# A transformer-style block on one core: the second matrix product runs three half steps behind the first, its passes in a new order, and the splitting of operands moves from GpSimd to ScalarE and VectorE

## The chip, the cores and the metric

The kernel runs on one core of a Trainium2 chip. The time is what one execution takes on the device, in microseconds (us). The engines of a core run side by side, each with its own queue of instructions in a fixed order, and wait for each other by semaphores: TensorE (PE, matrix products into PSUM), VectorE (DVE), ScalarE (ACT), GpSimd (POOL) and SyncE (SP, which only issues DMAs here). In a profile PEld stands for the loading of weights into TensorE.

## The reference

Two blocks follow each other. The first is an attention with a polynomial sketch: for 4 batches and 4 heads of 1088 tokens with 32 features, queries and keys are projected with S1 and S2 (8 x 32), the two projections multiplied pairwise to 64 features, and

```python
kv = np.einsum('bhsf,bhsd->bhfd', k_p, v)
z = np.sum(k_p, axis=2)
num = np.einsum('bhsf,bhfd->bhsd', q_p, kv)
den = np.einsum('bhsf,bhf->bhs', q_p, z)[..., None] + 1e-06
return (num / den)
```

Its result, as 4352 tokens of 128 features, is the input x of the second block, a mixture of E = 4 experts with F = 1024 hidden features, all in float32:

```python
p = domain_probs / (domain_probs.sum(-1, keepdims=True) + 1e-09)
for e in range(E):
    h = np.maximum(x @ w1[e], 0.0)
    out += p[:, e:e + 1] * (h @ w2[e])
```

## The kernel before, in words

The 4352 tokens are cut into 11 chunks (`CHUNKS`, line 71): 128, 448, 512 six times, 320, 256 and 128. A chunk takes 16 steps; a step `i` is a chunk `m` and a number `kq` that stands for an expert `e` and a pair `f` of blocks of 128 hidden features. So an expert takes four steps, and a step has two half steps, `j` = 0 and 1, each with one block of hidden features. The main loop (line 1084) goes through the steps and writes the order of all engines' instructions by hand; nothing reorders it later. Chunk 0 and the last are "plain" (whole fp32 products, tokens on the other side of the array). Chunk 1 is "whole": plain fp32 products for all four experts.

From chunk 2 on an fp32 product is put together from faster passes. Tokens and weights are split into rounded parts a and b and a correction d, held in the type fp32r. The first product of a half step, in `first`, has three passes: xa with wa (line 911), xb with wb (912), and, after ScalarE has scaled the sum in PSUM by 1 + 2^-12 (913), xd with wd (931). The third pass stands in `third`, one half step later, behind the first two passes of the next half step, so that ScalarE's scaling lies beside other passes. In what follows these three passes, two of a half step and the third of the one before, are called a trio. `third` also makes the hidden values. Of the even blocks (`in_three`) it makes three parts: ha by ScalarE (935), hb and hd by VectorE (936 and 937; the code calls the last one hc). Of the odd blocks it makes a single fp32 tile hid by ScalarE (943).

The second product, in `second`, multiplies the hidden values of an even block in three passes, ha and hb into one PSUM bank (o0, lines 994 and 995) and hd into another (o1, 1001), and of an odd block in one fp32 product into o1 (1001 too). That fp32 product counts as two instructions in the profile and takes as long as about four passes. `second` runs two steps behind `first` (`LA`), that is four half steps: `between` puts it after the trios. In the last step of an expert (`closing`) both halves are put after the first trio, so that the expert's end, `close`, comes early, and nothing stands after the second trio.

`close` calls `gather` (1022): ScalarE copies o0 out of PSUM with a scale (1030), VectorE adds o1 (1031), GpSimd multiplies by the gates of the tokens and adds to the chunk's total (1035 to 1038). o0 and o1 have one buffer each, so the next expert's first pass into a bank waits for that copy. ev, ob and total have one buffer each too.

The splits of weights (`weight_parts`, `second_weight_parts`) are spread over steps 16 to 39 by `to_part`, those of the tokens of a chunk (`token_parts`) are made in step 12 of the chunk before. ScalarE makes rounded copies (706, 717, 734, 758) and GpSimd subtracts (710).

The attention of the later batches runs beside all this in small pieces (`front`), most of them on VectorE. `work` hands them out evenly after each half step's first product, by what the next chunks need; at step 12 of a chunk what is still missing for the next one is made at once.

Of the kernel before, what the change touches and what calls it, by code (L numbers as in the profile page):

```python
# [8 lines left out]
F32 = mybir.dt.float32  # L9
# [15 lines left out]
def kernel(  # L25
# [673 lines left out]
    wb = cpool.tile([P, E, F], F32R, name="wb")  # L699
    wd = cpool.tile([P, E, F], F32R, name="wd")  # L700

    def scaled(tag, w, scale, dtype=F32):

        t = mpool.tile([P, CW], F32, tag=tag, bufs=1, name="tw")[:, :]
        t = t[:, 0 : w.shape[-1]]
        nc.scalar.activation(t.bitcast(dtype), w, ACTF.Copy, scale=scale)
        return t

    def minus(out, in0, in1):
        nc.gpsimd.tensor_tensor(out=out, in0=in0, in1=in1, op=ALU.subtract)  # L710

    def weight_parts(e):

        HF = F // 2
        for c in (slice(0, HF), slice(HF, F)):
            w, a, b, d = (x[:, c] for x in (w1_of[e], wa[:, e], wb[:, e], wd[:, e]))
            nc.scalar.activation(a, w, ACTF.Copy, scale=4096.0 * NEAR)
            minus(b, scaled("ob", w, 4096.0), a.bitcast(F32))
            yield
            minus(d, b.bitcast(F32), scaled("ev", w, NEAR, F32R))  # L720
            yield


# [3 lines left out]
    def second_weight_parts(e):  # L727

        w = w2_of[e, 0]
        vab = cpool.tile([P, 2, KS * NK * DM], F32R, tag=f"w1_{e}", name="vab")  # L730
        a, b = vab[:, 0], vab[:, 1]
        minus(b, scaled("ob", w, 4096.0), scaled("ev", w, 4096.0 * NEAR, F32R))
        yield
        nc.scalar.activation(a, w, ACTF.Copy, scale=NEAR)
        d = cpool.tile([P, KS * NK * DM], F32R, tag=f"w2_{e}0", name="vd")[:, :]
        minus(d, b.bitcast(F32), a.bitcast(F32))
        w2_parts[e] = a, b, d
        yield

# [13 lines left out]
    def token_parts(m):  # L753

        n = CHUNKS[m]
        xa, xb, xd_ = (mpool.tile([P, CW], F32R, tag=f"x{i}", name=f"x{i}") for i in "abd")
        ((x, _, _),) = placed(START[m], n)
        nc.scalar.activation(xa[:, 0:n], x, ACTF.Copy, scale=R12 * NEAR)
        minus(xb[:, 0:n], x, scaled("ew", x, NEAR, F32R))
        minus(xd_[:, 0:n], xa[:, 0:n].bitcast(F32), xb[:, 0:n].bitcast(F32))  # L760
        xparts[m] = xa, xb, xd_

    def start():

# [76 lines left out]
    def plain(m):  # L841
        return m in (0, NC - 1)

    def whole(m):
        return m == 1

    begun_hp, made_hp = {}, {}

# [12 lines left out]
    def first(i, work, between=None):  # L861
# [29 lines left out]
            work()  # L891
            return
        hid[i] = []
        if whole(m):
            ((x, _, _),) = placed(START[m], n)
            for j in range(2):
                hp = psum(ps_h, "h")[:, 0:n]
                nc.tensor.matmul(hp, w1_of[e][:, P * (2 * f + j) : P * (2 * f + j + 1)], x, start=True, stop=True)
                u = hidden()[:, 0:n]
                nc.scalar.activation(u, hp, ACTF.Relu)  # L900
                hid[i].append(u)
                work()
                if between and j == 0:
                    between(0)
            return
# [39 lines left out]
    def second(i, j=None):  # L945
# [4 lines left out]
        if plain(m):  # L950
# [27 lines left out]
        if whole(m):  # L978
# [7 lines left out]
        if f == 0 and j in (0, None):  # L986
            acc[m, e] = psum(ps_o, "o0"), psum(ps_o, "o1")
        o0, o1 = (o[:, 0:n] for o in acc[m, e])
        for j in range(2) if j is None else (j,):
            k = 2 * f + j  # L990
            if in_three(k):
                w = slice(DM * split_at(k), DM * (split_at(k) + 1))
                (va, vb, vd), (ha, hb, hc) = w2_parts[e], hd[j]
                nc.tensor.matmul(o0, va[:, w], ha, start=(k == 0), stop=False)  # L994
                nc.tensor.matmul(o0, vb[:, w], hb, start=False, stop=(k == FB - SK + KS - 1))  # L995
                o1_next.append((vd[:, w], hc))
            else:
                o1_next.append((second_weight(e, k), hd[j]))
            if k:
                for x, (w, h) in enumerate(o1_next):  # L1000
                    nc.tensor.matmul(o1, w, h, start=(k == 1 and x == 0), stop=(k == FB - 1 and x == len(o1_next) - 1))  # L1001
                o1_next.clear()

    o1_next = []

    def turn_back(m, src):

# [14 lines left out]
    def gather(m, e):  # L1022

        n = CHUNKS[m]
        ev = mpool.tile([P, CW], F32, tag="ev", bufs=1, name="ev")
        o0, o1 = acc.pop((m, e))
        if o0 is None:
            nc.scalar.copy(ev[:, 0:n], o1[:, 0:n])
        else:
            nc.scalar.activation(ev[:, 0:n], o0[:, 0:n], ACTF.Copy, scale=1.0 + R12)  # L1030
# [37 lines left out]
        begun_hp[i] = psum(ps_h, "h")  # L1068
        half_columns(i, begun_hp[i], 0)
    to_part = {}  # L1070
    for e in range(E):
        for at, parts_of in ((NQ + 4 * e, weight_parts(e)), (NQ + 8 + 4 * e, second_weight_parts(e))):
            for x in range(4):
                to_part.setdefault(at + x, []).append(parts_of)
    ending = iter(())

    def close(i):

        nonlocal ending
        ended = gather(steps[i][0], steps[i][1] // NP)  # L1080
        next(ended)
        ending = chain(ending, ended)

    for i in range(len(steps) + LA):
        if i < len(steps):
# [15 lines left out]
                    credit[0] -= 1  # L1101
                    piece()

            parted = i >= LA and not plain(steps[i - LA][0]) and not plain(m)
            closing = parted and steps[i - LA][1] % NP == NP - 1

            def between(j):

                if closing:
                    second(i - LA)  # L1110
                    close(i - LA)
                else:
                    second(i - LA, j)

            first(i, work, between if parted else None)
            for parts_of in to_part.get(i, ()):
                next(parts_of, None)
            if kq == NQ - 4 and 0 < m < NC - 2:
                while have[0] < START[m + 1] + CHUNKS[m + 1]:
                    piece()  # L1120
                token_parts(m + 1)
            if i == 2:
                gate_quotients()
            elif i == 5:
# [12 lines left out]
        if i >= LA:  # L1137
            parted = i < len(steps) and parted
            mm, kk = steps[i - LA]
            if parted and closing:  # L1140
                continue
            second(i - LA, 1 if parted else None)
            if kk % NP == NP - 1 and not plain(mm):
                close(i - LA)
            else:
                next(ending, None)

# [1 line left out]
_INS = ["q", "k", "v", "S1", "S2", "moe_domain_probs", "moe_w1", "moe_w2"]  # L1149
# [26 lines left out]
```

## Time and profile before

| what | us |
|---|---|
| time, median of 3 runs | 485.01 (484.96 to 485.11) |
| the profiled execution's own time | 485.2 |
| its span, first to last instruction | 483.4 |
| PE busy | 471.4 (98%) |
| VectorE busy | 327.2 (68%) |
| ScalarE busy | 331.2 (69%) |
| GpSimd busy | 141.9 (29%) |
| chunk 1, by the first products' starts | 29.4 to 81.0 |
| chunk 2 | 81.0 to 138.5 |
| chunks 3 to 7 | 138.5 to 404.6 |
| chunks 8 and 9 | 404.6 to 464 |

A row of the timeline has the start and the length in us, the engine, the line of the code, the instruction, what it writes and reads, and in brackets how long the engine stood idle before it and which instruction ended that. The ends of matmuls are modelled and overlap; their starts show the pace. The granted TensorE clock was full throughout.

### The profile page before, as it was taken

The numbers are of one execution on the slowest core, as the hardware profiler recorded it, in microseconds if no ns is written. First come the engines' busy times: TensorE is split into PE (matmuls) and PEld (weight loads), VectorE is DVE, ScalarE is ACT, GpSimd is POOL, SyncE is SP. The second block draws the span as 40 slices with busy tenths as digits, with TensorE's granted clock in tenths as the row PEclk, the third lists the DMA queues.
The fourth block names the chain that finished last, engine by engine and source line by source line (L and its number), as shares of the span: only waits on it lengthen the run. The fifth ranks groups of instructions, "written<-read, shape, count | busy, mean of one in ns | idle before, by whom it ended". The sixth has DMA issues, their size and how long they took to land.

```text
span 483.4 us, 8071 instructions
## 1 busy us (share of the span) xinstructions
PE 471.4 (98%) x2845; PEld 330.8 (68%) x2845; DVE 327.2 (68%) x615; ACT 331.2 (69%) x696; POOL 141.9 (29%) x149
## 2 busy tenths in 40 slices
PE   8999999989999999999999999999999999999997
PEld 5965555656666676666666676667666666888987
DVE  6833250696877769687887669597877686765652
ACT  4366676876857777676857777676877686888841
POOL 5134478432222124211322124212331032232120
PEclk9999999999999999999999999999999999999999
DMA  7827204411101212411103210013102100120710
GB/s 225 273 69 159 66 22 87 97 42 23 44 23 49 45 44 65 118 24 41 41 23 65 45 33 24 22 17 45 38 24 58 29 14 15 34 57 22 244 34 18
DMA packets 45472, 29.19 MB, mean 60 GB/s; under 512 B 26264, under 2 KB 40952, under 8 KB 45432
## 3 DMA queue, kind: packets, MB, share of 16 engines
q1 hardware_dynamic: 45416, 28.68, 23.6%
q8 instruction: 22, 0.36, 0.3%
q14 instruction: 18, 0.15, 0.1%
q10 hardware_dynamic: 16, 0.00, 0.0%
HBM read 24.42 MB, written 4.24 MB: 59 GB/s over the span
## 4 chain that ended last, share of the span: by engine, by line
PE 66%; DVE 6%; ACT 5%; issue 2%; ACTq 0%; DVEq 0%
PE o L1001 23%; PE h L931 10%; PE h L912 8%; PE h L911 8%; PE o L994 5%; PE o L995 5%; ACT h L913 3%; PE n L226 2%; PE h L226 2%; PE o L226 1%; DVE qp L535 1%; DVE hd L937 1%; DVE kp L425 1%; PE f L666 1%; DVE hb L936 1%
## 5 line engine op out<-in xcount | busy, mean ns | idle before, releaser
L913 ACT ACTIVATE h<-h 128x512 f32<-128x512 f32 (+2 forms) x256 | 138.0, 539 | 100.6 <-PE h L912 91.6
L936 DVE SCALAR_TENSOR_TENSOR hb<-h,ha 128x512 fp32r<-128x512 f32 (+2 forms) x128 | 80.8, 631 | 92.3 <-ACT ha L935 91.8
L911 PE MATMUL h<-xa,wa 128*128 128x512 f32 (+2 forms) x256 | 140.5, 549 | 0.0
L1001 PE MATMUL o<-hid,w_sb 128*128 128x512 f32 (+2 forms) x256 | 119.2, 547 | 0.0
L937 DVE SCALAR_TENSOR_TENSOR hd<-ha,hb 128x512 fp32r<-128x512 f32 (+2 forms) x128 | 98.8, 772 | 8.4
L931 PE MATMUL h<-xd,wd 128*128 128x512 f32 (+2 forms) x256 | 98.3, 384 | 3.2 <-ACT h L913 1.5
L912 PE MATMUL h<-xb,wb 128*128 128x512 f32 (+2 forms) x256 | 94.2, 368 | 0.0
L1037 POOL TENSOR_TENSOR ev<-ev,gate 128x512 f32<-128x512 f32 (+3 forms) x27 | 31.3, 1159 | 153.8 <-DVE ev L1031 153.1
L943 ACT ACTIVATE hid<-h 128x512 f32<-128x512 f32 (+2 forms) x128 | 70.2, 548 | 0.2 <-PE h L931 0.2
L935 ACT ACTIVATE ha<-h 128x512 fp32r<-128x512 f32 (+2 forms) x128 | 69.9, 546 | 0.0
L911 PEld LDWEIGHTS h<-xa,wa 128*128 128x128 f32 x256 | 48.2, 188 | 30.1 <-issue 18.6
L912 PEld LDWEIGHTS h<-xb,wb 128*128 128x128 f32 x256 | 48.3, 189 | 29.3 <-issue 23.6
L931 PEld LDWEIGHTS h<-xd,wd 128*128 128x128 f32 x256 | 48.0, 188 | 23.7 <-ACT h L913 16.0
L1001 PEld LDWEIGHTS o<-hid,w_sb 128*128 128x128 f32 x256 | 45.9, 188 | 8.1
L1001 PE MATMUL o<-hd,vd 128*128 128x512 f32 (+2 forms) x128 | 48.3, 378 | 2.7 <-DVE ev L1031 2.7
L994 PE MATMUL o<-ha,vab 128*128 128x512 f32 (+2 forms) x128 | 50.6, 395 | 0.0
L995 PE MATMUL o<-hb,vab 128*128 128x512 f32 (+2 forms) x128 | 47.4, 370 | 0.0
L1038 POOL TENSOR_TENSOR total<-total,ev 128x512 f32<-128x512 f32 (+3 forms) x27 | 35.4, 1313 | 2.1
L535 DVE TENSOR_TENSOR qp<-qa,qb 64x512 f32<-64x512 f32 (+5 forms) x44 | 33.1, 753 | 1.0
L1035 POOL TENSOR_TENSOR total<-ev,gate 128x512 f32<-128x512 f32 (+3 forms) x9 | 10.5, 1163 | 70.3 <-issue 34.0
L1001 PEld LDWEIGHTS o<-hd,vd 128*128 128x128 f32 x128 | 24.0, 187 | 9.3 <-DVE ev L1031 4.5
L984 PE MATMUL o<-hid,w_sb 128*128 128x448 f32 x64 | 28.9, 544 | 0.0
(150 smaller groups left out, 545.4 us busy)
## 6 DMA issues: line engine op xcount, KB each, us to landing
gate<-gates SPq DMA_DIRECT2D x16, 256.0 KB
kn<-in_k_dram SPq DMA_DIRECT2D x4, 544.0 KB
vn<-in_v_dram SPq DMA_DIRECT2D x16, 128.0 KB
w_sb<-in_moe_w_dram SPq DMA_DIRECT2D x4, 512.0 KB
w_sb<-in_moe_w_dram SPq DMA_DIRECT2D x8, 256.0 KB
w_last<-in_moe_w_dram SPq DMA_DIRECT2D x4, 512.0 KB
gate<-gates SPq DMA_DIRECT2D x8, 224.0 KB
qn<-in_q_dram SPq DMA_DIRECT2D x2, 544.0 KB
```

The costliest lines, as they stand in the source:

```text
L535: nc.vector.tensor_tensor(out=qp[p][64 * x : 64 * x + 64, 0:n], in0=qa[64 * p : 64 * p + 64, 0:n], in1=qb[64 * p : 64 * p + 64, 0:n], op=A ...
L911: nc.tensor.matmul(g, wa[:, e, w], xa, start=True, stop=False)
L912: nc.tensor.matmul(g, wb[:, e, w], xb, start=False, stop=True)
L913: nc.scalar.activation(g, g, ACTF.Copy, scale=1.0 + R12)
L931: nc.tensor.matmul(g, w, x, start=False, stop=True, skip_group_check=True)
L935: nc.scalar.activation(ha, g, ACTF.Relu, scale=NEAR)
L936: nc.vector.scalar_tensor_tensor(out=hb, in0=g, scalar=0.0, in1=high, op0=ALU.max, op1=ALU.subtract)
L937: nc.vector.scalar_tensor_tensor(out=hc, in0=high, scalar=R12, in1=hb.bitcast(F32), op0=ALU.mult, op1=ALU.subtract)
L943: nc.scalar.activation(hid[i][j], g, ACTF.Relu)
L994: nc.tensor.matmul(o0, va[:, w], ha, start=(k == 0), stop=False)
L995: nc.tensor.matmul(o0, vb[:, w], hb, start=False, stop=(k == FB - SK + KS - 1))
L1001: nc.tensor.matmul(o1, w, h, start=(k == 1 and x == 0), stop=(k == FB - 1 and x == len(o1_next) - 1))
```

## The change

The change has four parts.

- `behind` and the list `due` take the place of `LA` for the chunks that are not plain: the second product of a half step is put three half steps after its first product. No step has an exception at the end of an expert any more.
- `second` deals its passes out anew. In the first half step of an expert only ha is multiplied, in the second only hb (`o0_next`). The hd pass waits in `o1_next` until the next even block's turn, and the first odd block's fp32 product waits too. So o1 is first written two half steps after o0. The eviction of o0 by ScalarE moves from `gather` into `second`, right after the last hb pass (`evs`).
- The pieces of weights and tokens are made by ScalarE (`split`) and VectorE (`join`) alone. `join` forms an exact difference in one instruction, so that the second rounded copy falls away. The weights' splits are given out in the order of experts 2, 3, 0, 1, and tokens are split over steps 12 and 13.
- In chunk 1 only experts 0 and 1 are computed whole; experts 2 and 3 are computed in three passes, so that chunk 1's tokens are split as well, in steps 4 and 5 of chunk 1.

The diff, cut to its core:

```diff
-    def minus(out, in0, in1):
-        nc.gpsimd.tensor_tensor(out=out, in0=in0, in1=in1, op=ALU.subtract)
+    def split(a, w, scale):
+        nc.scalar.activation(a, w, ACTF.Copy, scale=scale * NEAR)
+
+    def join(out, in0, scale, in1, op):
+        nc.vector.scalar_tensor_tensor(out=out, in0=in0, scalar=scale, in1=in1, op0=ALU.mult, op1=op)
...
-            nc.scalar.activation(a, w, ACTF.Copy, scale=4096.0 * NEAR)
-            minus(b, scaled("ob", w, 4096.0), a.bitcast(F32))
-            yield
-            minus(d, b.bitcast(F32), scaled("ev", w, NEAR, F32R))
+            split(a, w, 4096.0)
+            join(b, w, -4096.0, a.bitcast(F32), ALU.add)
+            yield
+            join(d, a.bitcast(F32), -R12, b.bitcast(F32), ALU.subtract)
...
-        nc.scalar.activation(xa[:, 0:n], x, ACTF.Copy, scale=R12 * NEAR)
-        minus(xb[:, 0:n], x, scaled("ew", x, NEAR, F32R))
-        minus(xd_[:, 0:n], xa[:, 0:n].bitcast(F32), xb[:, 0:n].bitcast(F32))
+        split(xa[:, 0:n], x, R12)
+        join(xb[:, 0:n], xa[:, 0:n].bitcast(F32), 4096.0, x, ALU.subtract)
         xparts[m] = xa, xb, xd_
+        yield
+        join(xd_[:, 0:n], xa[:, 0:n].bitcast(F32), 1.0, xb[:, 0:n].bitcast(F32), ALU.add)
+        yield
...
-    def whole(m):
-        return m == 1
+    def whole(m, e):
+        return m == 1 and e < E // 2
...
+        if j == 0:
+            for args in o1_next:
+                into(1, *args)
+            o1_next.clear()
+            w = slice(DM * split_at(k), DM * (split_at(k) + 1))
+            (va, vb, vd), (ha, hb, hc) = w2_parts[e], hd[j]
+            into(0, va[:, w], ha)
+            if f == 0:
+                o0_next.append((vb[:, w], hb))
             else:
-                o1_next.append((second_weight(e, k), hd[j]))
...
+                into(0, vb[:, w], hb, f == NP - 1)
+            o1_next.append((vd[:, w], hc))
+            if f == NP - 1:
+                evs[m, e] = mpool.tile([P, CW], F32, tag="ev", bufs=1, name="ev")
+                nc.scalar.activation(evs[m, e][:, 0:n], acc[m, e][0][:, 0:n], ACTF.Copy, scale=1.0 + R12)
+            return
+        for args in o0_next:
+            into(0, *args)
+        o0_next.clear()
+        x = second_weight(e, k), hd[j]
+        if f == 0:
+            o1_next.append(x)
+        else:
+            if f == NP - 1:
+                for args in o1_next:
+                    into(1, *args)
                 o1_next.clear()
-
-    o1_next = []
+            into(1, *x, f == NP - 1)
...
+    for x, e in enumerate((2, 3, 0, 1)):
+        for at, parts_of in ((NQ + 4 * x, weight_parts(e)), (NQ + 4 + 4 * x, second_weight_parts(e))):
+            for step in range(at, at + 4):
+                to_part.setdefault(step, []).append(parts_of)
+    for m in range(1, NC - 1):
+        at, tokens = NQ * m - 4 if m > 1 else NQ + 4, token_parts(m)
+        for step in (at, at + 1):
+            to_part.setdefault(step, []).append(tokens)
...
+    def behind(at):
+
+        was = closed[0]
+        while due and due[0][0] <= at:
+            _, i, j = due.pop(0)
+            second(i, j)
+            m, kq = steps[i]
+            if kq % NP == NP - 1 and j == 1:
+                close(i)
+        return closed[0] != was
...
+            first(i, work, lambda j: behind(2 * i))
+            due.extend([(2 * i + 5, i, None)] if plain(m) else [(2 * i + 3, i, 0), (2 * i + 4, i, 1)])
...
+        if not behind(2 * i + 1):
+            next(ending, None)
```

Here `into(o, w, h, last)` issues one pass into bank o, and starts the bank's sum where it is the bank's first. `second_weight_parts` is rewritten with `split` and `join` in the same way as `weight_parts`.

In the new file the passes of the first product stand at lines 910, 911 and 930, ScalarE's scaling at 912, ha, hb, hd and hid at 934, 935, 936 and 942, all passes of the second product at 991, the eviction of o0 at 1011, the addition of o1 at 1053, `split` at 703 and `join` at 706.

More of the change, by code (lines that the diff above doesn't have):

```diff
@@ L700 @@
     wd = cpool.tile([P, E, F], F32R, name="wd")
[L702 to L707, printed above, removed]
-    def minus(out, in0, in1):
-        nc.gpsimd.tensor_tensor(out=out, in0=in0, in1=in1, op=ALU.subtract)
+    def split(a, w, scale):
+        nc.scalar.activation(a, w, ACTF.Copy, scale=scale * NEAR)
+    def join(out, in0, scale, in1, op):
+        nc.vector.scalar_tensor_tensor(out=out, in0=in0, scalar=scale, in1=in1, op0=ALU.mult, op1=op)
     def weight_parts(e):
@@ L731, in second_weight_parts @@
         a, b = vab[:, 0], vab[:, 1]
-        minus(b, scaled("ob", w, 4096.0), scaled("ev", w, 4096.0 * NEAR, F32R))
+        split(a, w, 4096.0)
+        join(b, w, 4096.0, a.bitcast(F32), ALU.subtract)
         yield
-        nc.scalar.activation(a, w, ACTF.Copy, scale=NEAR)
+        split(a, w, 1.0)
         d = cpool.tile([P, KS * NK * DM], F32R, tag=f"w2_{e}0", name="vd")[:, :]
-        minus(d, b.bitcast(F32), a.bitcast(F32))
+        join(d, b.bitcast(F32), 1.0, a.bitcast(F32), ALU.subtract)
         w2_parts[e] = a, b, d
@@ L893, in first @@
         hid[i] = []
-        if whole(m):
+        if whole(m, e):
             ((x, _, _),) = placed(START[m], n)
@@ L977, in second @@
             return
-        if whole(m):
+        if whole(m, e):
             if f == 0 and j == 0:
@@ L985, in second, with into @@
             return
-        if f == 0 and j in (0, None):
+        if f == 0 and j == 0:
             acc[m, e] = psum(ps_o, "o0"), psum(ps_o, "o1")
[L988 to L996, printed above, removed]
-            else:
-                o1_next.append((second_weight(e, k), hd[j]))
-            if k:
-                for x, (w, h) in enumerate(o1_next):
-                    nc.tensor.matmul(o1, w, h, start=(k == 1 and x == 0), stop=(k == FB - 1 and x == len(o1_next) - 1))
+            begun_o[:] = [False, False]
+        k = 2 * f + j
+        def into(o, w, h, last=False):
+            nc.tensor.matmul(acc[m, e][o][:, 0:n], w, h, start=not begun_o[o], stop=last)
+            begun_o[o] = True
+        if j == 0:
[7 more added lines that the diff above has]
+                o0_next.append((vb[:, w], hb))
+            else:
+                into(0, vb[:, w], hb, f == NP - 1)
[14 more added lines that the diff above has]
+                    into(1, *args)
                 o1_next.clear()
-    o1_next = []
+            into(1, *x, f == NP - 1)
+    o0_next, o1_next, begun_o, evs = [], [], [False, False], {}
     def turn_back(m, src):
@@ L1024, in gather @@
         n = CHUNKS[m]
-        ev = mpool.tile([P, CW], F32, tag="ev", bufs=1, name="ev")
         o0, o1 = acc.pop((m, e))
         if o0 is None:
+            ev = mpool.tile([P, CW], F32, tag="ev", bufs=1, name="ev")
             nc.scalar.copy(ev[:, 0:n], o1[:, 0:n])
         else:
-            nc.scalar.activation(ev[:, 0:n], o0[:, 0:n], ACTF.Copy, scale=1.0 + R12)
+            ev = evs.pop((m, e))
             nc.vector.tensor_tensor(out=ev[:, 0:n], in0=ev[:, 0:n], in1=o1[:, 0:n], op=ALU.add)
@@ L1070 @@
     to_part = {}
[L1071 to L1074, printed above, removed]
+    for x, e in enumerate((2, 3, 0, 1)):
[6 more added lines that the diff above has]
+            to_part.setdefault(step, []).append(tokens)
     ending = iter(())
@@ L1082, in close @@
         ending = chain(ending, ended)
+        closed[0] = i
+    due, closed = [], [None]
+    def behind(at):
[7 more added lines that the diff above has]
+        return closed[0] != was
     for i in range(len(steps) + LA):
@@ L1102, in work @@
                     piece()
[L1104 to L1117, printed above, removed]
+            first(i, work, lambda j: behind(2 * i))
+            due.extend([(2 * i + 5, i, None)] if plain(m) else [(2 * i + 3, i, 0), (2 * i + 4, i, 1)])
             if kq == NQ - 4 and 0 < m < NC - 2:
@@ L1120 @@
                     piece()
-                token_parts(m + 1)
+            for parts_of in to_part.get(i, ()):
+                next(parts_of, None)
             if i == 2:
@@ L1136 @@
                 half_columns(3, made_hp[3], c)
[L1137 to L1146, printed above, removed]
+        if not behind(2 * i + 1):
+            next(ending, None)
 _INS = ["q", "k", "v", "S1", "S2", "moe_domain_probs", "moe_w1", "moe_w2"]
```

## The prediction

> **What bounds the kernel now.** I read the page first, then the table of windows, then the timeline of the steady state, and last the timeline where a step is longer than its neighbours. The page:
>
> ```profile
> span 483.4 us, 8071 instructions
> ...
> PE 471.4 (98%) x2845; PEld 330.8 (68%) x2845; DVE 327.2 (68%) x615; ACT 331.2 (69%) x696; POOL 141.9 (29%) x149
> ...
> PEclk9999999999999999999999999999999999999999
> ```
>
> TensorE (PE) is busy 98% at full clock and no other engine is over 69%. But a matmul's end is modelled, so a short stall hides in "busy". Starts do not hide it. The timeline of PE in a stretch of chunk 7 without attention work, one row per step (first pass of the second product):
>
> ```profile
> 377.50 0.39 PE L994 MATMUL o<-ha,vab 128*128 128x512 f32 x1
> ...
> 380.45 0.40 PE L994 MATMUL o<-ha,vab 128*128 128x512 f32 x1
> ...
> 383.40 0.40 PE L994 MATMUL o<-ha,vab 128*128 128x512 f32 x1
> ...
> 386.65 0.39 PE L994 MATMUL o<-ha,vab 128*128 128x512 f32 x1
> ...
> 389.58 0.39 PE L994 MATMUL o<-ha,vab 128*128 128x512 f32 x1
> ```
>
> Steps of 2.95, 2.95, 3.25 and 2.93 us: an expert takes 12.08, four undisturbed steps 11.80, so each end of an expert costs 0.28. The same rows in chunk 8 (320 tokens) give 1.85 a step and 7.82 an expert (0.41 lost), in chunk 9 (256) 1.51 and 6.44 (0.40 lost). What is lost shows in the timeline at such an end, all engines:
>
> ```profile
> 212.42 0.39 PE L912 MATMUL h<-xb,wb 128*128 128x512 f32 x1
> ...
> 212.91 0.58 ACT L913 ACTIVATE h<-h 128x512 f32<-128x512 f32 x1 [0.74 <-PE h L912]
> ...
> 213.54 0.19 PEld L931 LDWEIGHTS h<-xd,wd 128*128 128x128 f32 x1 [0.47 <-ACT h L913]
> ```
>
> The third pass of a hidden block can start 1.13 us after its second (212.42 to 213.55), because ScalarE (ACT) scales PSUM in between. One pass is 0.234 us (L994 204.73, L995 204.96, L1001 205.20). At the end of an expert only four passes lie from one start to the other, 0.94 us: 0.19 is waited.
>
> The windows, here the second half of chunk 1, chunk 2 and chunk 4 (stretch, length, busy time of PE, PEld, DVE, ACT, POOL with counts, clock, DMA):
>
> ```profile
> 53.40:81.00 27.60, 27.60 (x120) 14.97 (x118) 7.33 (x14) 18.54 (x40) 19.96 (x16) 1.00 0.15 35
> 81.00:138.50 57.50, 54.06 (x269) 35.49 (x269) 42.58 (x70) 41.71 (x80) 22.80 (x17) 1.00 0.26 63
> 193.70:247.80 54.10, 52.95 (x245) 35.34 (x244) 43.17 (x73) 37.26 (x70) 12.86 (x9) 1.00 0.22 53
> ```
>
> Chunk 1 leaves VectorE (DVE) nearly idle and loads POOL; from chunk 2 on DVE works 43 of 54 us. Chunks 2 to 7 take 323.6 us (80.98 to 404.56) against 283.2 (96 steps of 2.95), 6.7 of ends of experts and about 24.1 of attention matmuls (rows of the timeline: 1.12 for 36 key sums, 1.15 for 32 query products, 0.88 for a projection, and so on): 9.6 are other stalls. Most lie where POOL's subtractions run beside DVE:
>
> ```profile
> 99.93 1.65 POOL L710 TENSOR_TENSOR vab<-tw 128x512 fp32r<-128x512 f32 x1 [7.14 <-ACT tw L706]
> ...
> 100.45 1.68 DVE L535 TENSOR_TENSOR qp<-qa,qb 64x512 f32<-64x512 f32 x1
> ...
> 102.75 0.50 PE L931 MATMUL h<-xd,wd 128*128 128x512 f32 x1 [0.63 <-ACT h L913]
> ```
>
> L535 takes 0.68 alone (98.35) and 1.68 here, the extra being 1.0 us.
>
> **The change part by part.** The sum is made against the profiled execution, 485.2 us (span 483.4 and 1.8 around it); the median is 485.01, 0.2 less.
>
> (1) Experts 2 and 3 of chunk 1 in three passes. A plain fp32 step there starts every 3.00 to 3.01 us (L898 at 37.09 and 40.09). A three-pass step of 448 tokens, on the line from 320 (1.85) to 512 (2.95), is 2.58. Eight steps by 0.43: **-3.4**. Bounds: 0 if ACT or DVE takes it back, which is (4), and 8 x (3.01 - 1.85 x 448/320) = -3.4 again by scaling alone.
>
> (2) The new order of passes. After the trio of an expert's first half step comes one pass (ha), after the second one (hb), and the error passes and plain fp32 passes move to the half steps behind. Between second and third pass there are now five passes, 1.17 us, against 1.13 needed: the wait goes. Two half steps of 0.94 follow each other while ACT issues two instructions 0.50 apart in each (L913 204.69, L943 205.19), so ACT falls back 0.06; I leave 0.04 a time. 24 experts of 512: 24 x 0.24 = 5.8. At 256 the two starts are 0.80 apart (459.98 to 460.78) and five passes 0.59: 0.21 stays, 0.19 is won; at 320, between the two, 0.88 needed and 0.71 there: 0.17 stays, 0.24 is won. Four of each: 1.7. Together **-7.5**; bounds 0 (ACT late at every end) and -10.0 (24 x 0.28 + 4 x 0.41 + 4 x 0.40). The second o bank is written again two half steps after its last pass, which also ends the ten waits for L1031 (2.7 on PE, 4.5 on its weight loads); their price is in the 9.6 and is not counted here. The eviction of o0 (L1030, 0.60) moves to the half step before; it waits for the last hb pass, and ACT's next scaling, queued behind it, is ready 0.45 later and issues 0.5 after it: nothing.
>
> (3) Pieces off POOL. Forty subtractions leave POOL (24 of weights, 16 of tokens) and 52 ACT instructions become 25; 42 come to DVE (chunk 1's tokens are new). In chunks 2 to 7 stalls of 8.2 us of the 9.6 lie beside a subtraction on POOL: 2.7 at 101.5, 1.8 at 130, 0.8 at 184.7, 1.5 at 286.9, 1.4 at 239.5. A collision costs DVE 1.0; the piece itself costs DVE 0.62 (L937, 93.44 to the next at 94.06). So 38% of 8.2 is won: **-3.0**. Bounds: -9.6, all stalls gone, and +11.2, eighteen pieces from chunk 2 on at 0.62 each on the path; between, the collisions are the nearest row. POOL keeps its gate products (1.28 and 1.30), which collide as before.
>
> The row says DVE loses 1.0 of a 1.65 us POOL instruction. The Trainium skill (SBUF — State Buffer, Who interferes with whom) says more, that the loser of the shared port is blocked for the whole instruction; at 1.65 the share won would be 62%, 5.1 us, and the sum 473.9. The skill also speaks against the change (Perfetto Trace Analysis, Optimizing Scalar/DVE Operations): work moved between GpSimd and VectorE may not help, as they share a port; then this term is nothing and the sum 479.0.
>
> (4) What the same move costs chunk 1. All weights are now split from step 16 to 33, expert 2 first. In the second half of chunk 1 DVE has, beside the 7.3 us of the window and 2.2 of turns that stood before it, 8 pairs of hb and hd (1.2 a pair at 448 tokens), 14 pieces at 0.62 and an eviction of 0.6: 28.4. PE has 27.6 - 3.4 = 24.2 there. ACT has 49 instructions, 22 us at their distances of 0.43 to 0.52. So DVE is the bound. Followed by hand in the order of the built program, with these durations, PE waits eight times: five times for a scaling queued on ACT behind splits, copies or the eviction (0.5, 0.45, 1.0, 0.1, 0.55), once for the turned keys (0.8), once for the eviction of o1 on DVE (1.05), once for hb (0.8): 5.3. The stage before held 0.4. **+4.9**. Bounds: 0, as the pieces need only weights that are long there, and +11 where DVE also idles 1.03 us before each of eight hb (91.8 us in 89 waits in the table of waits).
>
> (5) Three half steps of lag instead of four. Counted from the start of the trio that holds its third pass, a steady hb was due at 5.4 us and ready at 2.6, 2.8 to spare; now the tightest is that of an expert's second pair. It too is ready at 2.6 (third pass at 0.46, ACT to 1.81, hb 0.69 and a release), but due at 3.86: 1.26 to spare. In 89 of 128 cases DVE stood idle before hb, on time; late ones are 0.95 (hb at 214.95, ha there at 214.00) and 1.5 (217.66 after 216.15). **0** while DVE has that cover; without it 0.2 to 0.5 an expert.
>
> SP's queue keeps its order but for one gate load. Sum: -3.4 - 7.5 - 3.0 + 4.9 = -9.0: 476.2 for the profiled run, **476.0** as a median.
>
> **Rivals.**
> - *Better.* Chunk 1's pieces run ahead (1.5 instead of 4.9) and every stall beside POOL goes (8.2): -17.6, 467.4. For it: DVE 7.3 of 27.6 there. Against: DVE's 28.4.
> - *The order does not do what it says.* One pass of cover leaves 0.04 us; if ACT is late by that much more at each end, (2) is nothing: 483.5. For it: L931 waited for L913 in 40 places (17.5 us with the weight loads). Against: ACT stood idle before 163 of 256 scalings, 0.56 us each.
> - *Slower.* VectorE is behind at the second pair's hb in every expert. At 0.38 us in each of 24 it eats the 9.0. At 0.6, as when each stands 1.86 late, just over the 1.51 seen: +14.4, 490.4. For it: lag cut, 18 pieces more. Against: 89 of 128 on time.
>
> **How the numbers follow.** Forecast 0.63, better 0.12, order useless 0.13, slower 0.12. 0.2% (1.0 us) is what a measurement of this kernel tells from no change. Faster: 0.63 + 0.12 + most of 0.13 = 0.86; same 0.03; slower 0.11. The forecast's own range, with (3) and (4) moved by half their bounds, is 471 to 481. The whole range, 469.0 to 483.5, goes on to the order being useless and half way into the better case.
>
> **What would show it.** (1) First three-pass step of chunk 1 near 54 us, steps of about 2.6. (2) An expert of chunk 7 in 11.8 to 11.9, L930 no longer waiting 0.47. (3) DVE's two-input instructions near 0.69 in chunk 2, whose length falls from 57.5 to about 54. (4) Chunk 2 starting near 82 instead of 81, with waits for ACT and DVE before it. (5) hb not among PE's releasers. The prediction is wrong if chunk 1 loses more than 10 us, or if hb stalls PE through chunks 2 to 7.

## The result and the profile after

The changed kernel takes 478.24 us (median, 478.15 to 478.77) against 485.0 us (484.96 to 485.11) of the kernel before: a ratio of 0.986, with a 95% interval of 0.985 to 0.988. That is 6.8 us less, where 9.0 were forecast (476.0; range 469.0 to 483.5).

The page of the changed kernel:

```profile
span 476.4 us, 8137 instructions
...
PE 466.6 (98%) x2869; PEld 334.6 (70%) x2869; DVE 349.2 (73%) x675; ACT 321.6 (68%) x685; POOL 91.9 (19%) x109
...
PEclk9999999999999999999999999999999999999999
```

POOL's 50 us are gone, and VectorE carries 22 more. TensorE's "busy" again says nothing of short stalls, so the starts have to say it. PE and its weight loads in the attention-free stretch of chunk 7, the ha passes (one per step) and the two late loads of that expert:

```profile
372.86 0.40 PE L991 MATMUL o<-ha,vab 128*128 128x512 f32 x1
...
375.81 0.40 PE L991 MATMUL o<-ha,vab 128*128 128x512 f32 x1
...
378.76 0.40 PE L991 MATMUL o<-ha,vab 128*128 128x512 f32 x1
...
379.42 0.19 PEld L930 LDWEIGHTS h<-xd,wd 128*128 128x128 f32 x1 [0.23 <-ACT h L912]
...
380.42 0.19 PEld L930 LDWEIGHTS h<-xd,wd 128*128 128x128 f32 x1 [0.24 <-ACT h L912]
...
381.44 0.80 PE L991 MATMUL o<-ha,vab 128*128 128x512 f32 x1
...
384.78 0.39 PE L991 MATMUL o<-ha,vab 128*128 128x512 f32 x1
```

From 372.86 to 384.78 an expert takes 11.92 us; before it took 12.08, and four undisturbed steps take 11.80. The one long wait at an expert's end (0.47) has become two short ones, behind the two half steps that have a single pass of cover. Each makes the pass behind it start 0.06 late (L930 at 379.47, the next at 379.76: 0.29 instead of 0.23).

The windows of the second half of chunk 1, of chunk 2 and of chunk 4 (stretch, length, busy time of PE, PEld, DVE, ACT, POOL with counts, clock, DMA):

```profile
53.60:82.40 28.80, 26.04 (x141) 18.63 (x140) 23.29 (x42) 22.50 (x49) 5.38 (x4) 1.00 0.24 60
82.40:137.20 54.80, 53.45 (x273) 36.24 (x272) 46.09 (x80) 36.96 (x71) 9.67 (x7) 1.00 0.22 53
190.90:244.20 53.30, 52.23 (x245) 35.22 (x244) 42.55 (x74) 36.41 (x69) 10.02 (x7) 1.00 0.21 50
```

Chunk 2 starts at 82.4 instead of 81.0 and is 2.7 us shorter, chunk 4 is 0.7 shorter. What PE itself waited for, in the table of waits (total, times, longest):

```profile
PE o L991 <- DVE ev L1053: 2.0, 4, 0.9
PE h L930 <- ACT h L912: 1.3, 3, 0.8
PE o L991 <- DVE hb L935: 0.8, 1, 0.8
```

The first row is the wait that step 2 of the prediction said would end: the first pass into o1 waits until VectorE has added the old o1 to ev (L1053). It was 2.7 us in five places before.

This table gives the chunks by the starts of their first products, in us, for this kernel and for those that the next section builds. "1a" is chunk 1 up to its ninth step, "1b" the rest. A chunk's stretch begins with second products of the chunk before, three half steps of them or four, so a change of the lag alone moves some work from one column to another.

| kernel | 1a | 1b | 2 | 3 | 4 | 5 | 6 | 7 | 8 | 9 |
|---|---|---|---|---|---|---|---|---|---|---|
| before | 24.00 | 27.58 | 57.55 | 55.19 | 54.11 | 53.75 | 52.16 | 50.81 | 32.67 | 26.54 |
| after | 24.41 | 28.75 | 54.81 | 53.66 | 53.37 | 52.25 | 51.40 | 50.34 | 32.15 | 26.56 |
| p_only | 24.00 | 27.11 | 55.44 | 54.42 | 53.29 | 52.79 | 52.15 | 50.81 | 32.81 | 26.54 |
| o_and_p | 24.75 | 27.11 | 55.30 | 53.70 | 53.39 | 52.27 | 51.40 | 50.34 | 32.13 | 26.58 |
| o_only | 24.75 | 28.18 | 63.25 | 54.98 | 53.97 | 53.90 | 51.69 | 50.50 | 32.46 | 26.58 |
| o_ew | 24.75 | 28.98 | 58.43 | 54.97 | 54.07 | 53.89 | 51.71 | 50.51 | 32.47 | 26.57 |
| lag4 | 24.00 | 27.11 | 54.33 | 55.97 | 56.50 | 53.91 | 52.14 | 50.27 | 33.33 | 27.01 |
| deal | 24.76 | 27.11 | 56.42 | 55.80 | 56.76 | 53.17 | 52.40 | 50.12 | 31.65 | 26.54 |
| swap | 24.75 | 27.11 | 54.05 | 55.34 | 52.98 | 52.38 | 51.33 | 50.34 | 32.15 | 26.56 |
| bare | 24.76 | 27.11 | 55.75 | 54.33 | 53.83 | 52.79 | 52.01 | 50.80 | 32.38 | 26.67 |

### The profile page after: what moved, and what is told of

It reads as the page before. It is cut to its first block, busy times and chain, and to the rows that moved or that the text cites. A ratio compares the mean times of both kernels' runs of the same rounds, so it can differ in the third digit from the quotient of the medians.

```text
span 476.4 us, 8137 instructions
## 1 busy us (share of the span) xinstructions
PE 466.6 (98%) x2869; PEld 334.6 (70%) x2869; DVE 349.2 (73%) x675; ACT 321.6 (68%) x685; POOL 91.9 (19%) x109
## 4 chain that ended last, share of the span: by engine, by line
PE 89%; DVE 5%; ACT 3%; issue 1%; DMA 1%; SPq 0%; ACTq 0%; DVEq 0%
PE o L991 38%; PE h L930 12%; PE h L911 11%; PE h L910 11%; PE h L226 4%; PE o L226 3%; PE n L226 3%; PE h L897 3%; PE o L983 2%; PE f L666 1%; DVE qp L535 1%; ACT h L912 1%; DMA kn<-in_k_dram 1%; PE f L410 1%; DVE hb L935 1%
## 5 line engine op out<-in xcount | busy, mean ns | idle before, releaser
L912 ACT ACTIVATE h<-h 128x512 f32<-128x512 f32 (+3 forms) x272 | 147.9, 544 | 110.5 <-PE h L911 109.8
L935 DVE SCALAR_TENSOR_TENSOR hb<-h,ha 128x512 fp32r<-128x512 f32 (+3 forms) x136 | 85.6, 629 | 82.3 <-ACT ha L934 81.5
L910 PE MATMUL h<-xa,wa 128*128 128x512 f32 (+3 forms) x272 | 137.4, 505 | 0.0
L991 PE MATMUL o<-hid,w_sb 128*128 128x512 f32 (+3 forms) x272 | 126.8, 548 | 0.0
L930 PE MATMUL h<-xd,wd 128*128 128x512 f32 (+3 forms) x272 | 106.0, 390 | 1.6 <-ACT h L912 1.3
L936 DVE SCALAR_TENSOR_TENSOR hd<-ha,hb 128x512 fp32r<-128x512 f32 (+3 forms) x136 | 99.7, 733 | 10.3 <-DVE hb L935 1.4
L911 PE MATMUL h<-xb,wb 128*128 128x512 f32 (+3 forms) x272 | 100.3, 369 | 0.0
L942 ACT ACTIVATE hid<-h 128x512 f32<-128x512 f32 (+3 forms) x136 | 75.1, 552 | 0.2 <-PE h L930 0.2
L934 ACT ACTIVATE ha<-h 128x512 fp32r<-128x512 f32 (+3 forms) x136 | 74.6, 549 | 0.0
L911 PEld LDWEIGHTS h<-xb,wb 128*128 128x128 f32 x272 | 51.3, 188 | 25.9 <-issue 19.1
L930 PEld LDWEIGHTS h<-xd,wd 128*128 128x128 f32 x272 | 51.0, 187 | 22.3 <-ACT h L912 14.6
L991 PE MATMUL o<-ha,vab 128*128 128x512 f32 (+3 forms) x136 | 62.6, 460 | 0.0
```

What stands on the lines that cost most here:

```text
L910: nc.tensor.matmul(g, wa[:, e, w], xa, start=True, stop=False)
L911: nc.tensor.matmul(g, wb[:, e, w], xb, start=False, stop=True)
L912: nc.scalar.activation(g, g, ACTF.Copy, scale=1.0 + R12)
L930: nc.tensor.matmul(g, w, x, start=False, stop=True, skip_group_check=True)
L934: nc.scalar.activation(ha, g, ACTF.Relu, scale=NEAR)
L935: nc.vector.scalar_tensor_tensor(out=hb, in0=g, scalar=0.0, in1=high, op0=ALU.max, op1=ALU.subtract)
```

## The experiments

The first four kernels take the change apart: the order of passes with its lag (o), the pieces on ACT and VectorE (p), the three passes in chunk 1 with the new order of the weights' splits (w). The kernel before, timed again beside these, took 485.44 us; beside the later groups it took 485.2 to 485.6.

### o_only and o_ew: the order alone

Out of the changed kernel the new pieces, chunk 1's three passes and the new order of the weights' splits are taken back (the diff is cut):

```diff
-        split(a, w, 4096.0)
-        join(b, w, 4096.0, a.bitcast(F32), ALU.subtract)
+        minus(b, scaled("ob", w, 4096.0), scaled("ev", w, 4096.0 * NEAR, F32R))
...
-        return m == 1 and e < E // 2
+        return m == 1
```

> The new order of passes and the lag of three half steps alone; pieces on GpSimd as before, chunk 1 whole as before. As predicted (step 2): -7.5 us against the kernel before, 477.5, an undisturbed expert of 512 tokens in 11.84 us. By the changed kernel's trace, where such an expert takes 11.92, one of 320 tokens 7.76 and one of 256 tokens 6.54: 24 x -0.16, 4 x -0.06, 4 x +0.10, together -3.7, 481.3. Rival: the stalls beside GpSimd's subtractions were in truth waits for the second bank, which the order ends; then the order alone brings nearly all of the 6.8, about 478.

490.81 us, a ratio of 1.011 (1.010 to 1.012): 5.4 slower. Chunk 2 alone is 5.7 longer. The timeline of o_only there, all engines:

```profile
99.81 0.63 DVE L1034 STREAM_TRANSPOSE ob<-total 128x448 f32<-128x448 f32 x1
...
100.46 1.94 SPq L1037 DMA_DIRECT2D out_dram<-ob  x4
...
103.93 1.15 ACT L706 ACTIVATE tw<-w_sb 128x512 f32<-128x512 f32 x2 [3.24 <-DVE qa L679]
105.16 1.26 POOL L710 TENSOR_TENSOR vab<-tw 128x512 fp32r<-128x512 f32 x1 [10.89 <-ACT tw L706]
106.45 0.60 ACT L1013 ACTIVATE ev<-o 128x512 f32<-128x512 f32 x1 [1.37 <-POOL vab L710]
106.95 0.59 ACT L914 ACTIVATE h<-h 128x512 f32<-128x512 f32 x1
...
107.59 0.80 PE L932 MATMUL h<-xd,wd 128*128 128x512 f32 x1 [4.90 <-ACT h L914]
```

ACT's scratch copy for POOL (L706) is written into the buffer "ob", out of which the four output transfers (L1037) are still reading; the scaling of h (L914) is queued behind it, and PE waits 4.9 us for that. The profile puts ACT's 3.24 us down to a VectorE shuffle that ended just then. To tell a buffer from the order, o_ew gives that copy another buffer:

```diff
-            minus(b, scaled("ob", w, 4096.0), a.bitcast(F32))
+            minus(b, scaled("ew", w, 4096.0), a.bitcast(F32))
```

> o_only with one edit: the scaled copy for POOL's b pieces goes into the buffer of the token scratch instead of the one that the output's turned block uses (the same ACT copy, the same POOL subtraction, no added work). Theory: o_only lost 5.7 us in its second chunk because ACT's scratch copy had to wait 3.2 us for the output's transfers out of that buffer, with the scaling of h queued behind it (PE then waited 4.9 us for the scaling), which says nothing of the order of passes. Then the second chunk comes back from 63.25 us to about 57.5, PE's one wait of 4.9 us is gone, and the whole is 484 to 485, about 5.5 below o_only, near before. Rival: the three half steps of lag and the new order overload ACT in the second chunk whatever the buffers are; then it stays within 1 us of o_only's 490.8.

487.17 us against 485.2 (1.004, 1.003 to 1.005). Chunk 2 falls from 63.25 to 58.43: the buffer was 4.8 of the 5.7. But the order alone is still 2.0 us slower than before; 484 to 485 was expected. What PE waits for in o_ew:

```profile
PE o L993 <- DVE ev L1055: 4.2, 5, 1.2
PE h L932 <- ACT h L914: 3.4, 4, 2.0
```

With POOL's pieces in place the addition out of o1 comes later than before (4.2 us against 2.7) and ACT is behind in chunks 1 and 2. The longest wait for ACT is again a buffer:

```profile
104.55 0.60 ACT L1013 ACTIVATE ev<-o 128x512 f32<-128x512 f32 x1 [1.83 <-POOL vab L710]
...
105.68 0.50 PE L932 MATMUL h<-xd,wd 128*128 128x512 f32 x1 [2.00 <-ACT h L914]
```

o_ew moves only the scratch copies that lay in "ob". Others still lie in "ev", which the eviction of o0 writes (L1013): it waits 1.83 us until POOL has read them, with the scaling (L914) behind it in ACT's queue. Chunks 1b and 2 lose 2.3 us in o_ew; chunks 3 to 7 win 0.9. No run takes the scratch copies out of "ev" as well, so what the order costs with POOL's pieces and no shared buffer stays open.

### p_only: the pieces alone

The kernel before with `split` and `join` in place of `scaled` and `minus`, old order, old lag, chunk 1 whole:

```diff
-        minus(b, scaled("ob", w, 4096.0), scaled("ev", w, 4096.0 * NEAR, F32R))
+        split(a, w, 4096.0)
+        join(b, w, 4096.0, a.bitcast(F32), ALU.subtract)
```

> The pieces of weights and tokens by ScalarE and VectorE, in the old order of passes with four half steps of lag and chunk 1 whole. As predicted (step 3): -3.0 us, 482.0. By the changed kernel's trace (chunks 2 to 7 shorter by 7.7, of which 3.9 are ends of experts): -3.8, 481.2. Rival (the end of the old order hides it): within 1 us of the kernel before, 485.

480.21 us, 0.989 (0.988 to 0.990): 5.2 faster. Chunks 2 to 5 are shorter by 0.8 to 2.1 each. The groups of instructions of VectorE between 80 and 140 us (busy time, mean ns of one, idle before) show one reason; the kernel before:

```profile
L535 DVE TENSOR_TENSOR qp<-qa,qb 64x512 f32<-64x512 f32 x4 | 4.7, 1180 | 0.1
L535 DVE TENSOR_TENSOR qp<-qa,qb 64x320 f32<-64x320 f32 x4 | 4.3, 1078 | 0.1
```

and p_only:

```profile
L535 DVE TENSOR_TENSOR qp<-qa,qb 64x320 f32<-64x320 f32 x4 | 2.9, 731 | 0.1
L535 DVE TENSOR_TENSOR qp<-qa,qb 64x512 f32<-64x512 f32 x4 | 2.7, 686 | 0.1
```

The same eight instructions take 5.6 us instead of 9.0, 3.4 less, which pays for most of the six pieces that VectorE makes itself in this stretch (0.67 to 0.69 each). VectorE's busy time there still rises, from 43.3 to 46.8 us, and ACT's falls from 43.8 to 40.3. In the whole trace PE's waits for VectorE's addition and its qp (L535) fall from 4.4 to 1.4 us, those for ACT's scaling from 1.5 to 0.7.

The second kind has another cause. In the kernel before, ACT's rows just ahead of the stall at 102.75 that the prediction shows are:

```profile
101.61 0.60 ACT L1030 ACTIVATE ev<-o 128x512 f32<-128x512 f32 x1 [0.76 <-POOL vab L710]
102.11 0.59 ACT L913 ACTIVATE h<-h 128x512 f32<-128x512 f32 x1
```

The eviction waits for POOL's subtraction, which reads a scratch copy in the same buffer "ev", and the scaling for which PE waits is queued behind it. p_only has no scratch copies. So collision, shared buffer and ACT's lighter load went together in p_only, and no run parts them.

### o_and_p and o_and_w: pairs

o_and_p is the changed kernel with chunk 1 whole and the weights' splits in their old order; o_and_w is the changed kernel with POOL's pieces.

```diff
 o_and_p
-        return m == 1 and e < E // 2
+        return m == 1
```

> Both, without experts 2 and 3 of chunk 1 in three passes. If chunk 1's part costs what the trace shows (chunk 2 starts 1.4 us later, 0.7 us less is left over from chunk 1), this is 0.7 us faster than the changed kernel, 477.5. As predicted (steps 1 and 4, +1.5): 476.7. Rival: chunk 1's part pays, by its 3.4 us: 481.6.

> The new order and experts 2 and 3 of chunk 1 in three passes, with the pieces on GpSimd as before (in the new order of experts). If VectorE's pieces are what takes back chunk 1's 3.4 us, chunk 1 is shorter here than in the changed kernel (chunk 2 starts before 80.5), and the stalls beside GpSimd's subtractions come back in chunks 2 to 7: 481.3 - 3.4 + 1 = 479. If ScalarE's queue takes it back, which has 27 instructions more here, chunk 2 starts at 82.5 or later: 481 to 483.

o_and_p takes 477.86 us (0.985, 0.983 to 0.986), a shade under the changed kernel. o_and_w takes 496.05 (1.022, 1.020 to 1.024); the second half of chunk 1 alone takes 38.64 us there. So the parts do not add up as separate terms: the order is worth -2.35 us on top of the new pieces and +2.0 without them (o_ew), and chunk 1's three passes cost little with the new pieces and 5.2 more than o_only without them. Part of this is the shared scratch: o_and_w still has both buffers, PE waits 11.7 us in eight places for ACT's scaling, and its mean granted clock was 0.986 to 0.993.

### bare, deal: how much cover the scaling needs

Both deal the passes of o_and_p once more. bare leaves nothing beside the first trio of an expert and puts ha and hb beside the second; deal puts ha and hb beside the first and the o1 passes of the first pair beside the second, so that no trio has a single pass of cover.

```diff
 bare
-            into(0, va[:, w], ha)
             if f == 0:
-                o0_next.append((vb[:, w], hb))
+                o0_next.extend([(va[:, w], ha), (vb[:, w], hb)])
             else:
+                into(0, va[:, w], ha)
+            if f:
                 into(0, vb[:, w], hb, f == NP - 1)
 deal
-            if f == 0:
-                o0_next.append((vb[:, w], hb))
-            else:
-                into(0, vb[:, w], hb, f == NP - 1)
+            into(0, vb[:, w], hb, f == NP - 1)
...
-        if f == 0:
-            o1_next.append(x)
+        if f in (0, NP - 1):
+            for args in o1_next:
+                into(1, *args)
...
```

> o_and_p with no pass at all beside the first trio of an expert and both passes of o0 beside the second: slots 0,2,7,4,3,4,3,5. It measures what a late weight load costs. Theory: the trio's third pass waits 0.47 us as at the end of each expert in the kernel before, and an expert of 512 goes from 11.92 to the 12.08 it had there: 24 x 0.16 = 3.8 if all shows, 2.3 if as much shows as of the order: 480.2 to 481.7. Rival: the order's gain comes from the lag or from the earlier eviction and not from the cover of the scaling: within 0.5 us of 477.9.

> o_and_p (new order and pieces by ACT and VectorE, chunk 1 whole, 477.9 us) with the eight slots of an expert dealt once more: both passes of o0 beside the first trio, the passes of o1 of the first pair beside the second, so in units of one fast pass 2,5,3,4,3,4,3,5 in place of 1,1,7,4,3,4,3,5. Theory: what the order still loses are the two late weight loads per expert (0.23 and 0.24 us at 512 tokens, costing 0.12 together; 0.25 each at 256) behind slots of one pass; with them gone an expert takes 11.80 instead of 11.92, 24 x 0.12 = 2.9, with some 0.6 in the 256-token and 0.3 in the 320-token chunk: 474.1 if all of it shows, 476 if the busy chunks show as little of it as they did of the order itself. Rival: o1 of the next expert now begins 8 passes (1.84 us) after the old one ended instead of 13, and VectorE's addition out of o1 (0.7 to 1.05 us, queued behind other work) is not done: PE then waits at the first pass into o1, 0.3 us or more an expert, 32 x 0.3 = 9.6 less 3.8: above 480.

bare: 481.3 us, 3.4 over o_and_p, within the 2.3 to 3.8 expected. The weight loads and ha passes of its quiet expert in chunk 7:

```profile
381.38 0.19 PEld L930 LDWEIGHTS h<-xd,wd 128*128 128x128 f32 x1 [0.47 <-ACT h L912]
...
381.72 0.39 PE L991 MATMUL o<-ha,vab 128*128 128x512 f32 x1
...
393.81 0.39 PE L991 MATMUL o<-ha,vab 128*128 128x512 f32 x1
```

The wait of 0.47 is back, and the expert takes 12.09, as before the change. So the cover is what the order's gain comes from.

deal: 485.58 us, 7.7 over o_and_p: the rival, not the theory. Where nothing else runs it wins (chunk 8 in 31.65 instead of 32.13, chunk 7 in 50.12 instead of 50.34), but PE waits for the addition:

```profile
PE o L991 <- DVE ev L1047: 9.7, 8, 2.6
```

o1 is needed again five passes earlier, and VectorE, which takes its instructions in order, has not come to the addition. Part of the 7.7 is the clock (last section): the one execution at a clock of 1.0 took 483.72.

### lag4: four half steps instead of three

o_and_p, with one line changed:

```diff
-            due.extend([(2 * i + 5, i, None)] if plain(m) else [(2 * i + 3, i, 0), (2 * i + 4, i, 1)])
+            due.extend([(2 * i + 5, i, None)] if plain(m) else [(2 * i + 4, i, 0), (2 * i + 5, i, 1)])
```

> o_and_p with the second product four half steps behind instead of three, its passes dealt as in o_and_p. Theory (step 5 of the prediction): hb is in time with three, so a fourth half step is worth nothing: 477.9 within 1 us. Rival: hb and the late work of ACT and VectorE hold PE in busy chunks, which is why the order gave 2.3 and not 3.7 to 7.5; then a longer lag wins 1.5 us or more (476.4 or below), most of it in chunks 2 to 5.

485.48 us: 7.6 slower, which neither theory had. hb is not late. PE's waits for the addition are 6.2 us in eight places, against 1.8 in four. With 2.1 us in two waits for attention's fs (L410) and about 1.1 of the clock (last section) that makes the 7.6. VectorE's timeline in chunk 9, where no attention runs, around the addition; lag4:

```profile
447.67 0.42 DVE L935 SCALAR_TENSOR_TENSOR hb<-h,ha 128x256 fp32r<-128x256 f32 x1
448.20 0.42 DVE L936 SCALAR_TENSOR_TENSOR hd<-ha,hb 128x256 fp32r<-128x256 f32 x1
448.54 0.41 DVE L1053 TENSOR_TENSOR ev<-ev,o 128x256 f32<-128x256 f32 x1
```

and o_and_p:

```profile
445.05 0.43 DVE L935 SCALAR_TENSOR_TENSOR hb<-h,ha 128x256 fp32r<-128x256 f32 x1 [0.61 <-ACT ha L934]
445.58 0.42 DVE L936 SCALAR_TENSOR_TENSOR hd<-ha,hb 128x256 fp32r<-128x256 f32 x1
445.92 0.42 DVE L1053 TENSOR_TENSOR ev<-ev,o 128x256 f32<-128x256 f32 x1
```

In o_and_p the expert's last pass (hid into o1) starts at 445.12 and takes 0.59: the addition starts 0.2 after its end. In lag4 that pass starts at 446.90 and the addition 1.05 after its end, because the hb and hd of the same half step stand ahead of it in VectorE's queue and wait for ACT. An expert closes in a first half step with a lag of three and in a second one with a lag of four, and only the second one's `third` makes hb and hd.

In chunk 9 this costs nothing: an expert takes 6.50 us there and 6.54 in o_and_p. Chunks 3 to 5 take 7.0 us more. Between the end of the expert's last pass and the longest wait (2.62 us, ended at 241.68) VectorE's queue holds hb and hd (238.13 and 238.92), but also a shuffle and two products of attention and a piece of tokens. That hb and hd make the difference there is argued from the queue; no run moves the closing alone at a lag of four.

### swap, deal_swap, after_swap, deal4_swap: the addition ahead of the attention work

The second product's passes, and with them the closing, are written ahead of the half step's share of attention work, in o_and_p, deal and the changed kernel:

```diff
-            work()
             if between and j == 0:
                 between(0)
+            work()
```

> o_and_p with one order turned round: in the first half of each step the second product's passes, and with them the closing of an expert and its addition out of o1 on VectorE, are issued ahead of that half step's share of attention work instead of behind it. Theory: the addition that PE waits for (1.8 us in four places of o_and_p, 6.2 in eight of lag4, 9.7 in eight of deal) is late because VectorE takes its instructions in order and attention's instructions of 0.7 us each stand ahead of it; one to three of them less ahead brings each of these waits down by 0.7 to 2 us: o_and_p's four waits go, 1.0 to 2.0 us less, 476 to 477. Rival: VectorE is behind in these stretches altogether, and what is moved behind the addition is waited for next (qp, the keys); then 477.9 within 0.5.

> deal with the same turning round. Theory: deal's 7.7 us over o_and_p are the shorter room for the addition out of o1 (eight waits of 0.3 to 2.6 us, 9.7 in all) against 3.8 won at the late weight loads; with the addition ahead of the half step's attention work at least two thirds of the 9.7 go: 485.6 to 479 or below. Rival: passes beside the first two trios (the scaling) or another wait made deal slow; then it stays above 484.

> The changed kernel (with two experts of chunk 1 in three passes, 478.2 us) with the same turning round. Theory: its four waits for the addition out of o1 (0.72, 0.24, 0.20, 0.87 us) go, and it falls by as much as swap does against o_and_p, 476.3 to 477.3. It also tells whether the three passes in chunk 1 are still worth nothing (0.4 us more than without) when the addition is early.

deal_swap takes 478.25 us: the turn gives back 7.3 of the 7.7 that deal had lost, so VectorE's order it was. swap stays at 477.85, the rival, and after_swap at 478.73, where 476.3 to 477.3 were expected. In swap the waits for the addition are gone and others stand in their place:

```profile
PE o L991 <- DVE hb L935: 2.7, 3, 1.4
```

Behind the longest of them VectorE has just worked 3.03 us without a gap on two of attention's products of keys (L425, from 181.23), and hb comes after. So the turn changes which of VectorE's products PE waits for, and not the time; that no order could do better is not shown.

A last kernel joins deal's dealing, four half steps of lag and the turn in both halves:

```diff
-            if between and j == 0:
-                between(0)
+            if between:
+                between(j)
...
-            first(i, work, lambda j: behind(2 * i))
+            first(i, work, lambda j: behind(2 * i + j))
```

> deal_swap with the second product four half steps behind, its passes (and the closing) ahead of the half step's attention work in both halves. Theory: what holds PE in deal_swap are VectorE's hb (2.8 us in four waits) and its addition out of o1 (2.3 in four), both by the order of VectorE's queue; a half step more gives hb three to eight passes (0.7 to 1.8 us) more, so the hb waits go and the total falls to 475 to 476, below every kernel so far. Rival: VectorE is saturated around the ends of chunks 2 to 4, so that any order pays some 2 us there: 477.5 to 479, with the waits moved to the addition out of o1 or to attention's operands.

490.31 us, the slowest with the new pieces, above both expectations. Its waits:

```profile
PE o L991 <- DVE ev L1047: 13.2, 22, 2.0
```

22 places, quiet ones too: the hb and hd of the closing half step are ahead of the addition again (in chunk 9 at 449.42 and 449.95, the addition at 450.29), and where no attention runs the turn moves nothing. No kernel here beats o_and_p and swap, and they stand 0.4 us under the changed kernel, less than can be told apart.

## Why the prediction came out as it did

The sign, the range and the main case held. Two of the five steps were mis-sized, in opposite senses, and the step on the lag asked only half its question.

**(1) and (4), chunk 1, together +1.5 forecast: right in sense, smaller.** Three passes against whole products in chunk 1 cost 0.9 us in one comparison on the same chip (after_swap against swap) and 0.4 by the medians of after and o_and_p. The first three-pass step runs from 53.65 to 56.16, 2.5 us, as step 1 said (2.58), and the waits of step 4 came where they were put, but not as many. PE's timeline in the changed kernel has, among five of over 0.2 us:

```profile
73.35 0.47 PE L930 MATMUL h<-xd,wd 128*128 128x448 f32 x1 [0.76 <-ACT h L912]
75.66 0.48 PE L930 MATMUL h<-xd,wd 128*128 128x448 f32 x1 [0.33 <-ACT h L912]
82.09 0.47 PE L991 MATMUL o<-hb,vab 128*128 128x448 f32 x1 [0.81 <-DVE hb L935]
```

The five come to 2.7 (with 0.24 and 0.58 at 59.6 and 60.7); the walk had 5.3 in eight. By the starts they cost more: the pass at 73.35 stands 1.13 behind the one before it, where 0.20 is the pace, so 0.93 is lost and not 0.76. VectorE was busy 23.3 us there, not the 28.4 of the step.

**(2), the order, -7.5 forecast, -2.35 on top of the pieces: the term that failed.** Three errors are in it. First, 0.04 was left for each expert; the measured loss is 0.06 at each of its two half steps with one pass, 0.12 in all, so an expert wins 0.16 and not 0.24, 24 x 0.16 = 3.8 instead of 5.8. Second, the sentence that two half steps more of room "ends" the waits for the addition out of o1: 1.8 us of them remain in o_and_p, 0.5 were there in p_only, and the difference of 1.3 is as large as what lies between 3.8 and the 2.5 that chunks 2 to 7 gained. Third, the experts of 320 and 256 tokens won nothing together, where 1.7 was forecast: one of 320 takes 7.76 instead of 7.82, one of 256 takes 6.54 instead of 6.44. At 256 L930's load waits 0.25 once an expert, behind the single pass, but deal has no such wait there and takes 6.53 too; what lengthens these steps stays open. The table's 0.75 more in 1a and much of the 0.64 less in chunks 8 and 9 are work that moved: with the lag of three 1a holds 26 instructions of the second product (L983, o_and_p), with four (lag4) 24, and its 24.00 is back.

**(3), the pieces, -3.0 forecast, -5.2 measured.** Right in the main, share too small, and one row misread. The step priced a collision by one VectorE instruction's extra 1.0 us and took 38% of the 8.2 us of stalls. Chunks 2 to 7 went from 323.6 to 318.9, so 4.7 of the 8.2 went, 57%. Most of the waits that went were for VectorE, as the step has it (4.4 us to 1.4). But the stall at 102.75, which the step shows beside a collision, is a wait for ACT behind the shared buffer "ev"; the step had no term for that. The Trainium skill's page (SBUF — State Buffer, Who interferes with whom), whose whole blocked instruction gave 62% and 5.1, was nearer than my row. The other rule weighed (the Trainium skill, Perfetto Trace Analysis, Optimizing Scalar/DVE Operations) says only that such a move may give nothing; p_only gained 5.2. That the ratio comes out near does not show the port rule itself: ACT lost half of its splitting copies, all scratch copies among them, in the same edit.

**(5), the lag, 0 forecast.** For hb it holds: from chunk 2 on hb is not among PE's releasers in the changed kernel. But the step asked only about hb. With the new dealing the lag decides in which half of a step an expert closes, and so what stands ahead of the addition in VectorE's queue; lag4 is 7.6 us slower, all but about 1.1 of it waits. The old kernel, with four, had its closing in the first half step by an exception; its waits for the addition were 2.7 us.

**The sum.** -5.2 - 2.35 + 0.4 to 0.9 is -6.7 to -7.2; measured were 6.8. That these add up is no finding, as each was measured on top of the one before; without the new pieces the other two parts together make the kernel 10.6 us slower (o_and_w). And that the forecast came within 2.2 us is in part luck: the gain of the order was priced 5.1 too high, that of the pieces 2.2 too low, and the cost of chunk 1 0.6 to 1.1 too high. The prediction treated (1), (2) and (3) as independent terms and none of its rivals said that one carries the others. Of the rivals, the useless order was nearest: less than a third of its 7.5 was won. The slower one (hb late in every expert) did not come in the changed kernel, and the better one had no room, since chunk 1 gained nothing.

## What to carry to other kernels

Where a fast engine is held by short-lived products of slower ones, list for each buffer that is written again the instructions that stand ahead of its releaser in that engine's queue; a change of lag by half a step can move it behind a pair that waits for a third engine. Parts of a change that load the same two queues are not to be priced one by one: ask what each part is worth without the others. And before an ordering is blamed for a stall, look for scratch buffers that share a tag with a tile that a transfer or another engine still reads or writes.

## What the runs showed of the hardware

After a wait of 2.6 us TensorE can run at a lower granted clock. The windows of lag4 around its longest wait, which ends at 241.68 (the number behind POOL's count is the clock, then come the DMAs' share and rate):

```profile
240.00:242.00 2.00, 0.32 (x1) 0.30 (x2) 1.99 (x4) 0.01 (x1) 0.30 (x1) 1.00 0.02 4
242.00:244.00 2.00, 2.00 (x4) 0.95 (x3) 1.49 (x2) 0.00 (x0) 1.92 (x2) 0.50 0.03 8
244.00:246.00 2.00, 2.00 (x13) 1.30 (x14) 0.00 (x0) 0.38 (x1) 0.65 (x1) 0.65 0.46 51
246.00:248.00 2.00, 2.00 (x35) 1.44 (x30) 1.16 (x2) 0.71 (x2) 0.00 (x0) 1.00 0.59 80
```

By the clock 1.7 us of work are lost there on top of the wait. Executions of lag4 with a mean clock of 1.0 take 484.2 to 484.5 us, those with 0.996 485.3 to 486.3, so a dip costs about 1.1. The 4.9 us wait of o_only is followed by windows at 0.60, 0.50, 0.50 and 0.70. It is no fixed rule: deal has the same dip after 2.23 us at 241.99 and none after 2.61 at 104.46, and a wait of 2.02 us in the profiled execution of deal4_swap, like one of 2.00 in o_ew, was followed by none; but three other executions of deal4_swap had a mean clock of 0.996 to 0.997. So the price of a long wait is its length and at times half as much again, while kernels with no wait over 1 us in the steady part (before, after, o_and_p) kept a mean clock of 0.999 to 1.0.

A weight load that came 0.23 us late cost 0.06 and not 0.23. Loads run ahead of their passes: the late one started 0.05 before its pass (379.42 and 379.47 above), others 0.23 before theirs (L911 in the same trace: 379.00 and 379.23). So waits of PEld are not to be added up as time lost.
